# Moving the first list load of a routed layer ahead of the last scatters, and 4 KB runs for three input loads

## The chip, the core and the metric

One core of a Trainium2 chip runs the whole program. The metric is the device time of one execution in microseconds (us). TensorE (PE) does the matrix products, VectorE (DVE) and ScalarE (ACT) the elementwise work, GpSimd (POOL) issues the indirect transfers, and SyncE (SP) issues the ordinary ones. Each engine works through its own instructions in the order in which they were written, and waits where an operand isn't ready.

## The reference, cut to what matters

```python
p_packed = sm_attn(p, k, v)              # 8 batches x 8 heads, 576 keys, 32 packed rows, head 64
x = sm_attn(q, p_packed, p_packed)       # -> 4608 tokens x 512
h = np.maximum(x @ w_in, 0.0)            # dense layer, 2048 wide
x = (h * h) @ w_out
noisy = x @ w_gate + log1p(exp(x @ w_noise)) * noise   # 8 experts
top2 = argpartition(-noisy, 2)[:, :2]; top2_w = softmax of the two
for e in range(8):                       # routed layer, 1024 wide, two experts per token
    out[mask_e] += top2_w * (np.maximum(x[mask_e] @ w1[e], 0) @ w2[e])
```

`w_in` and `w_out` come as 64-bit floats and are decoded on the core into pairs of 32-bit numbers.

## The kernel before

**Stages.** The dense layer runs in 16 blocks `j` of 288 tokens (two blocks make a batch of 576), each in 16 steps `f` of 128 hidden columns. A step is six matmuls on PE (line 655), the squared ReLU on ACT and DVE (lines 659 to 683), and, two steps later, twelve matmuls of the second product (line 691). Its second operand `gl` is made by DVE (line 682). The routed layer follows in tiles: each expert has three (512, 384 and 256 tokens, with 64 more for four of the experts), and a tile has eight steps.

**Routing.** After each batch `route(k)` finds for every token its two experts and its place in each expert's list, and writes (token, weight) into the DRAM tensor `lst` with scatters: twelve for a batch, one after the other on POOL (line 627), each waiting until the one before has landed. The last batch is routed in two halves, `route(7)` and `route(8)`, of six scatters each. After batch 5 the fullest expert so far is named the first one, and its first list (512 places) is taken as full; its second list (384 places) is full after batch 6.

**Lists, gathers, transposes.** `load_groups(k)` reads list `k` in the order of the gathers (four transfers into `lg0`, line 794), `group_index` turns that into row numbers `gi0` on DVE (line 800), and `load_list` reads it with the weights (four transfers into `ls0`, line 788). `gather` reads 32 token rows by `gi0` with one indirect transfer on POOL (line 837), 16 of them for tile 0 and 12 for tile 1. `trans_a` turns the gathered rows on DVE (line 845), `trans_b` splits them into two parts on ACT and DVE (lines 853 and 854), and the tile's matmuls (line 863) read those.

**The order.** Blocks 0 to 14, with the decode of the weights, the attention and the routing of batches 0 to 6, are ordered by a planner (`schedule`). It takes each `unit` with its engine, cost and dependences; where PE would idle in the first 45 us it inserts small matmuls (line 1113). A scatter costs 1040 ns on POOL there, and a transfer lands 1200 + 900 ns later. From block 15 on the order is written out by hand (lines 1125 to 1242). In block 15, step 0 loads list 0 and computes its index, step `SPL` does the same for list 1; `G0` places the gathers of tile 0 at steps 1 to 7 and 9, `T0` its transposes at steps 8, 11, 12 and 13. The weights of the first expert arrive through a two-buffer tile `wst` (`wload` on SP, `wsplit` on ACT and DVE), one per step. `RP` and `RR` are the half steps of block 15 at which the pieces of the logits and of `route(7)` stand; `SPEC` does the same for `route(8)` in tile 0.

**Input loads.** A chunk of `w_in` (512 KB) is read as 512 runs of 1 KB, 16 KB apart; one of `w_out` as 128 runs of 4 KB. `q` (576 KB for a block) is read in runs of 1152 bytes from four distant planes, `v` (512 KB and a rest of 64 KB) in neighbouring runs of 1 KB, `kT` (576 KB) in runs of 4608 bytes. Chunks go through three buffers `st`; the first four are the ones that this text speaks of most.

Of the kernel before, what the change touches and what calls it, by code (L numbers as in the profile page):

```python
# [12 lines left out]
I32 = mybir.dt.int32  # L13
# [8 lines left out]
P = 128  # L22
B, H, S, D = 8, 8, 576, 64
NPK = 32
NT, DM, FF = B * S, H * D, 2048
E, F2 = 8, 1024
BLK = 288
NB = NT // BLK
# [1 line left out]
RT = BLK // QP  # L30
KC = 5
XB = 6
SPL = 7
YS = 3
GF = 2
GLEAD = 2
# [10 lines left out]
NFF = FF // P  # L47
# [10 lines left out]
DUE = 9  # L58
RING = 8
JA = 2  # L60
RP = [5, 8]
RR = [11, 11, 13, 14, 16, 18, 18, 20, 22, 24, 26, 28, 30]
SPEC = [4, 5, 6, 6, 7, 8, 9, 9, 10, 10, 11, 14, 15, 15, 16, 17]
TILES = ((P, P, P, P), (P, P, P), (P, P))
EXTRA = P // 2
# [14 lines left out]
JSPEC = {B - 3: SIZE[0], B - 2: SIZE[0] + SIZE[1]}  # L80
# [2 lines left out]
TERMS = ((0, 0), (0, 1), (1, 0))  # L83


def program(ctx, tc, qT, kT, v, pT, w_in, w_out, wg, wn, noise, w1, w2, out):
    nc = tc.nc
    ctx.enter_context(tc.manual_schedule())
    dram = ctx.enter_context(tc.tile_pool(name="dram", bufs=1, space=DRAM))
# [42 lines left out]
    ls0 = cst.tile([P, BASE[2], 2], I32, name="ls0")  # L132
    lg0 = cst.tile([P, 4 * BASE[2], 2], I32, name="lg0")
    gi0 = cst.tile([P, 4 * BASE[2]], I32, name="gi0")
# [50 lines left out]
    raw = {}  # L185

    def load_raw(n):
        kind, i = chunks[n]
        raw[n] = stg.tile([P, 512, 2], I32, name="st", bufs=STB)
        if kind:  # L190
            nc.sync.dma_start(raw[n].rearrange("p a b -> p (a b)"), w_out[P * i:P * i + P].bitcast(I32))
        else:
            nc.sync.dma_start(raw[n].rearrange("p (c f) b -> p c (f b)", c=4),
                              w_in[:, P * i:P * i + P].bitcast(I32).rearrange("(c p) f -> p c f", p=P))

    units = {}

    def unit(name, eng, fn, deps, cost=60, dma=0, psum=(), dense=0.98):
        units[name] = (eng, cost, deps, fn, dma, psum, dense)
# [72 lines left out]
    def part1(n):  # L272
        b, quad = n // 2, n % 2
        st = {}
# [7 lines left out]
        def u_v():  # L282
            if n in LENT:
                w = win[:, 2:, FF - 512:].rearrange("p a (c d) -> p a c d", c=2)
                st["v"] = [w[:, c // 2, c % 2] for c in range(4)] + [win[:, 2, FF - 768:FF - 512]]
                for a in range(2):
                    nc.sync.dma_start(w[:, a], v[b, quad, 256 * a:256 * a + 256].rearrange("(c p) d -> p c d", p=P))
            else:
                w = p1.tile([P, KC, 256], F, name="vq", bufs=1)
                st["v"] = [w[:, c] for c in range(KC)]  # L290
                nc.sync.dma_start(w[:, :4], v[b, quad, :512].rearrange("(c p) d -> p c d", p=P))
            nc.sync.dma_start(st["v"][4][:64], v[b, quad, 512:])

        def u_s():
            st["s"] = [side(f"s1{i}", [P, 288]) for i in range(2)]
# [56 lines left out]
        x, y = ("A", n), ("A", n - 1)  # L352
# [61 lines left out]
    def part2(j):  # L414
        b = j // 2
        st = {}

        def u_l():
            st["q"] = att.tile([P, 4, BLK], F, name="q", bufs=QB)
            nc.sync.dma_start(st["q"], qT[:, :, j * BLK:(j + 1) * BLK].rearrange("g p t -> p g t"))  # L420

        def u_s():
            st["s"] = [side(f"s2{r}", [P, BLK]) for r in range(2)]
            heads(b, st["s"], st["q"])

        def u_m():
            a = att.tile([P, 2 * BLK], F, name="a2", bufs=1)
            for r in range(2):
                nc.vector.transpose(a[:, r * BLK:(r + 1) * BLK], st["s"][r])
            a = st["a"] = a.rearrange("p (x k) -> p x k", k=NPK)  # L430
            m = att.tile([P, 2 * BLK // NPK], F, name="m2", bufs=2)
            nc.vector.tensor_reduce(m, a, axis=AX.X, op=OP.max)
            nc.vector.tensor_sub(a, a, m.unsqueeze(2).to_broadcast([P, 2 * BLK // NPK, NPK]))

        def u_e():
            nc.scalar.activation(st["a"], st["a"], AF.Exp, scale=SCALE)

        def u_n():
            s = att.tile([P, 2 * BLK // NPK], F, name="sm2", bufs=2)
            a = st["a"]  # L440
            nc.vector.tensor_reduce(s, a, axis=AX.X, op=OP.add)
            nc.vector.tensor_scalar(s, s, 1e-9, None, op0=OP.add)
            nc.vector.reciprocal(s, s)
            nc.vector.tensor_mul(a, a, s.unsqueeze(2).to_broadcast([P, 2 * BLK // NPK, NPK]))

        def u_t():
            st["aT"] = att.tile([P, 2, BLK], F, name="aT", bufs=1)
            nc.vector.transpose(st["aT"].rearrange("p d t -> p (d t)"), st["a"].rearrange("p x k -> p (x k)"))

        def u_h():  # L450
            for i in range(2):
                xT[j, i] = mo.tile([P, 2, BLK], FR, name=f"xT{i}", bufs=2)
            act_copy(xT[j, 0], st["aT"])

        def u_d():
            nc.gpsimd.tensor_sub(xT[j, 1], st["aT"], xT[j, 0].bitcast(F))  # L456

        x, prev = ("Q", j), ("Q", j - 1)
        unit(x + ("l",), "sp", u_l, [("Q", j - QB, "s")], dma=393216)
        unit(x + ("s",), "pe", u_s, [x + ("l",), prev + ("t",), ("A", 2 * b, "y"), ("A", 2 * b + 1, "y")], 560,  # L460
             psum=(x + ("m",),) * 2, dense=0.89)
        unit(x + ("m",), "dve", u_m, [x + ("s",), prev + ("t",)], 2400)
        unit(x + ("e",), "act", u_e, [x + ("m",)], 620)
        unit(x + ("n",), "dve", u_n, [x + ("e",)], 2050)
        unit(x + ("t",), "dve", u_t, [x + ("n",), prev + ("h",), prev + ("d",)], 680)
        unit(x + ("h",), "act", u_h, [x + ("t",), ("M", j - 2, NFF - 1, "1")], 620)
        unit(x + ("d",), "pool", u_d, [x + ("h",)], 1500)
# [40 lines left out]
    def route(k):  # L508
        r0, n = ROUTES[k]
        st = {}  # L510
# [121 lines left out]
        rest = [u1, u1b, u1c, u2, u2b, u3, u3b] + [sc(r, i) for r in range(n) for i in range(2)]  # L632
        if k < B - 1:
            p = ("R", 2 * k + 1, "l")
            for i, (fn, eng, c) in enumerate(((u1, "dve", 250), (u1b, "act", 2700), (u1c, "dve", 1500),
                                              (u2, "dve", 2200), (u2b, "dve", 1700), (u3, "pe", 100), (u3b, "dve", 2000))):
                unit(("U", k, i), eng, fn, [p, ("U", k - 1, 6 + 4 * RT)], c, psum=(("U", k, 6),) if i == 5 else ())
                p = ("U", k, i)
            for i in range(4 * RT):
                unit(("U", k, 7 + i), "pool", rest[7 + i], [p], 1040, dma=64)  # L640
                p = ("U", k, 7 + i)
        if k == len(ROUTES) - 1:
            rest.insert(7, u3c)
        return rest
# [104 lines left out]
    def expert(e):  # L749
        if e not in reg:  # L750
            reg[e] = nc.sync.value_load(ordi[:1, min(e, 1), e:e + 1], min_val=0, max_val=E - 1)
        return bass.ds(reg[e], 1)
# [32 lines left out]
    def load_list(k, es, dst):  # L785
        src, n, r = list_rows(k, es)
        for g in range(n // 32):
            nc.sync.dma_start(dst[32 * g:32 * g + 32, :, BASE[k]:BASE[k] + r], src[g])

    def load_groups(k, es, dst):  # L790
        l = lst.rearrange("(e s) w -> e s w", e=E)[es, START[k]:START[k] + SIZE[k]]
        l = l.rearrange("e (j b) w -> j e b w", j=32)
        for a in range(4):
            nc.sync.dma_start(dst[32 * a:32 * a + 32], l)

    def groups(k):
        return slice(4 * BASE[k], 4 * BASE[k] + SIZE[k] // 32)

    def group_index(dst, src):
        nc.vector.tensor_scalar(dst, src, 4.0, pq4, op0=OP.mult, op1=OP.add)  # L800

    def by_rank(src, n, out=None):
        t = m2["a"].tile([P, 4, P], F, name="xs", bufs=2).rearrange("p a b -> p (a b)")[:, :(E - 1) * n * E]
# [321 lines left out]
    for i, (kind, j, f) in list(enumerate(steps))[NS * NFF:]:  # L1125
# [15 lines left out]
        if kind == 0 and j == NB - 1:  # L1141
            if f >= LAG - 1:
                wload(0, f - LAG + 1)
            for k, sl in enumerate((0, SPL)):
                if f == sl:
                    load_groups(k, expert(0), lg0[:, groups(k)].unsqueeze(1))
                    group_index(gi0[:, groups(k)], lg0[:, groups(k), 0])
                    load_list(k, expert(0), ls0.unsqueeze(1))
            for t, r, x in G0.get(f, ()):
                gather(t, r, x, x + 2)  # L1150
            if f in T0:
                trans_a(0, T0.index(f))
# [15 lines left out]
        else:  # L1168
# [28 lines left out]
            elif j + 1 < len(tiles):  # L1197
                if (j, f) in LST:
                    for k in LST[j, f]:
                        b = groups(abs(k) % 8)  # L1200
                        i = min(abs(k) % 8, 2)
                        b = slice(b.start - 4 * BASE[i], b.stop - 4 * BASE[i])
# [10 lines left out]
                if (j, f) in LGI:  # L1213
                    for k in LGI[j, f]:
                        if k < 0:
                            b = slice(4 * BASE[2], NG)
# [3 lines left out]
                        else:  # L1220
                            b = groups(k)
                            rank_groups(k, b.start, NG if k == 2 else b.stop)
                n = len(rows(j + 1))
# [27 lines left out]
    with tc.For_i(0, n_over, 1) as j:  # L1251
        with tc.tile_pool(name="sb3", bufs=1) as sb, tc.tile_pool(name="ps3", bufs=1, space=PSUM) as ps:
# [12 lines left out]
            for r in range(2):  # L1265
                g = sb.tile([P, DM], F, name="g", bufs=2)
# [11 lines left out]
            for r in range(2):  # L1278
# [3 lines left out]
                y = sb.tile([P, DM], F, name="y", bufs=2)  # L1282
# [36 lines left out]
```

## Time and profile before

| | us |
|---|---|
| median of 3 runs | 1714.87 |
| range of the runs | 1714.64 to 1718.84 |
| the profiled execution | 1713.52 |
| its span in the trace | 1711.7 |

Times in the rows below are counted from the span's start. The profiled execution lies 1.35 us under the median and outside its span has 1.8 us. PE is busy for 96% of the span.

### The profile page before, as it was taken

The page shows a single profiled execution, that of the slowest core. Times are in us where ns is not written, and L with a number is a line of the kernel's source. Part 1 is how long each engine was busy: PE and PEld are TensorE (multiplying, and loading weights), DVE is VectorE, ACT ScalarE, POOL GpSimd, SP SyncE. Part 2 cuts the span into 40 slices and gives each one's busy share as a digit, 9 for nine tenths or more (in the row PEclk, how much of TensorE's full clock was granted, in tenths as well). Part 3 has the DMA queues.
Part 4 walks back from the last instruction along what each step waited for, and adds up shares of the span by engine and source line. Part 5 has one row for each costly group of instructions (what it writes and reads, how often), then busy time and mean ns, then how long its engine had stood idle before and what let it go on. Part 6 is the DMA issues. An engine that isn't in the chain of part 4 may idle for free. (4 is left out here: it accounts for less than half of the span.)

```text
span 1711.7 us, 28563 instructions
## 1 busy us (share of the span) xinstructions
PE 1650.4 (96%) x11110; PEld 1430.0 (84%) x11110; DVE 877.4 (51%) x2040; ACT 640.9 (37%) x1372; POOL 537.0 (31%) x500
## 2 busy tenths in 40 slices
PE   8999999999999999995899799999999999999996
PEld 6669898989898998995788588888888888888886
DVE  6993757566665757572645544334343343433321
ACT  4775545344444444442623223222222232322211
POOL 0000020302011111204415636535365363645611
PEclk9999999999999999997999899999999999999998
DMA  8653132232322112102415535334253343534312
GB/s 243 189 156 79 29 95 70 69 97 69 96 67 79 48 53 58 29 15 59 95 24 122 112 58 120 74 83 96 62 104 84 73 108 68 111 75 92 69 25 32
DMA packets 143664, 140.80 MB, mean 82 GB/s; under 512 B 33071, under 2 KB 111919, under 8 KB 143527
## 3 DMA queue, kind: packets, MB, share of 16 engines
q1 hardware_dynamic: 120295, 100.05, 20.9%
q0 software_dynamic: 23232, 38.90, 13.3%
q8 instruction: 88, 1.44, 0.4%
q14 instruction: 49, 0.40, 0.1%
HBM read 99.71 MB, written 39.19 MB: 81 GB/s over the span
## 5 line engine op out<-in xcount | busy, mean ns | idle before, releaser
L691 PE MATMUL acc<-gh,wo 128*128 128x288 f32 x2048 | 426.1, 301 | 17.6 <-DVE x2T L698 17.6
L691 PEld LDWEIGHTS acc<-gh,wo 128*128 128x128 f32 x2048 | 330.0, 190 | 49.3 <-issue 22.4
L837 POOL DMA_INDIRECT xg<-x2d,gi x296 | 295.6, 999 | 107.6 <-issue 98.8
L870 DVE SCALAR_TENSOR_TENSOR hl<-ph,hh 128x512 fp32r<-128x512 f32 (+3 forms) x184 | 105.7, 575 | 433.7 <-ACT hh L869 433.6
L691 PE MATMUL acc<-gl,wo 128*128 128x288 f32 x1024 | 303.3, 296 | 1.6 <-DVE gl L682 1.5
L869 ACT ACTIVATE hh<-ph 128x512 fp32r<-128x512 f32 (+3 forms) x184 | 92.7, 504 | 484.8 <-PE ph L863 484.8
L655 PE MATMUL ph<-xT,ring 128*128 128x288 f32 x1536 | 246.4, 301 | 0.7 <-POOL xT L456 0.5
L627 POOL DMA_INDIRECT lst<-ent,pi x96 | 90.9, 947 | 483.9 <-DVE pi L606 248.0
L863 PE MATMUL ph<-ring,wb 128*128 128x512 f32 (+3 forms) x1152 | 225.0, 345 | 8.6 <-ACT ring L104 8.6
L655 PEld LDWEIGHTS ph<-xT,ring 128*128 128x128 f32 x1536 | 215.4, 189 | 19.2 <-ACT g L662 8.1
L892 POOL DMA_INDIRECT out<-y,ls x76 | 123.7, 1627 | 325.2 <-DVE y L889 158.4
L863 PE MATMUL ph<-ring,wo 128*128 128x512 f32 (+3 forms) x1152 | 222.0, 341 | 1.9 <-DVE hl L870 1.9
L863 PEld LDWEIGHTS ph<-ring,wb 128*128 128x128 f32 x1152 | 195.8, 189 | 32.6 <-ACT ring L104 9.0
L863 PEld LDWEIGHTS ph<-ring,wo 128*128 128x128 f32 x1152 | 194.0, 188 | 24.6 <-DVE hl L870 2.4
L691 PEld LDWEIGHTS acc<-gl,wo 128*128 128x128 f32 x1024 | 194.4, 190 | 2.9 <-DVE gl L682 2.9
L880 PE MATMUL acc<-wo,hh 128*128 128x512 f32 (+1 forms) x608 | 191.3, 396 | 0.0
L662 ACT ACTIVATE g<-ph 128x288 f32<-128x288 f32 x256 | 104.2, 407 | 221.0 <-PE ph L655 213.1
L880 PE MATMUL acc<-wb,hh 128*128 128x512 f32 (+1 forms) x576 | 179.5, 393 | 0.0
L677 DVE TENSOR_TENSOR g<-g 128x288 f32<-128x288 f32 x208 | 98.2, 472 | 129.3 <-ACT gh L668 128.9
L682 DVE TENSOR_TENSOR gl<-g,gh 128x288 fp32r<-128x288 f32 x256 | 123.4, 482 | 51.5 <-ACT gh L104 35.7
L880 PEld LDWEIGHTS acc<-wo,hh 128*128 128x128 f32 (+1 forms) x608 | 110.5, 185 | 22.7 <-issue 0.5
L880 PEld LDWEIGHTS acc<-wb,hh 128*128 128x128 f32 (+1 forms) x576 | 105.0, 185 | 20.6
(203 smaller groups left out, 1785.9 us busy)
## 6 DMA issues: line engine op xcount, KB each, us to landing
wst<-w SPq DMA_DIRECT2D x128, 256.0 KB, 3.0
out<-zero SPq DMA_DIRECT2D x37, 256.0 KB, 4.2
q<-qT SPq DMA_DIRECT2D x16, 576.0 KB, 4.7
x2d<-x2s SPq DMA_DIRECT2D x64, 144.0 KB, 2.7
kq<-kT SPq DMA_DIRECT2D x15, 576.0 KB, 3.8
st<-w_in SPq DMA_DIRECT2D x16, 512.0 KB, 7.7
st<-w_out SPq DMA_DIRECT2D x16, 512.0 KB, 4.2
vq<-v SPq DMA_DIRECT2D x15, 512.0 KB, 4.1
```

The lines of the kernel that those rows point to most:

```text
L627: nc.gpsimd.indirect_dma_start(out=lst, out_offset=bass.IndirectOffsetOnAxis(ap=st["pi"][:, r, k:k + 1], axis=0), in_=st["ent"][:, r, k], ...
L655: nc.tensor.matmul(ph, w[:, a, d], xT[j, b][:, d], start=n == 0, stop=n == 5)
L662: nc.scalar.activation(g, ph, AF.Relu)
L677: nc.vector.tensor_mul(g, g, g)
L682: nc.vector.tensor_sub(gl, g, gh.bitcast(F))
L691: nc.tensor.matmul(acc[j][d], wo[:, f, b, d * P:(d + 1) * P], g[a], start=f == 0 and n == 0, stop=f == NFF - 1 and n == 2)
L837: nc.gpsimd.indirect_dma_start(out=g[:, x], out_offset=None, in_=src, in_offset=bass.IndirectOffsetOnAxis(ap=idx, axis=0))
L863: nc.tensor.matmul(ph, wblock(e, f, a)[:, c], xt[t][b][:, c, :n], start=i == 0, stop=i == 11)
L869: nc.scalar.activation(hh, ph, AF.Relu)
L870: nc.vector.scalar_tensor_tensor(hl, ph, 0.0, hh.bitcast(F), op0=OP.max, op1=OP.subtract)
L880: nc.tensor.matmul(acc["e", t, r], h[a][:, o:o + n], wblock(e, 8 + f, b).rearrange("p c f -> p (c f)"), start=first and i == 0, stop=last ...
L892: nc.gpsimd.indirect_dma_start(out=out, out_offset=bass.IndirectOffsetOnAxis(ap=sl[:, 0:1], axis=0), in_=y, in_offset=None, compute_op=OP.add)
```

## The change

Three things change. **Lists:** the load of list 0 leaves step 0 of block 15 and becomes three units of the planner, behind the last scatter of batch 5 and ahead of the first scatter of batch 6: groups and list on SP, the index on DVE. The first scatters of batch 6 wait for both loads. List 1 is loaded at step 8 instead of 7, and its index stands two steps behind its load. **Routing slots:** the pieces of `route(7)` are spread anew over block 15. **Layouts:** the host lays out `w_in`, `v` (all but its last 64 rows) and `q` so that each partition reads one run of 4 KB (`q`: 4608 bytes).

```diff
-SPL = 7
+SPL = 8
-RP = [5, 8]
-RR = [11, 11, 13, 14, 16, 18, 18, 20, 22, 24, 26, 28, 30]
+RP = [5, 7]
+RR = [8, 8, 11, 12, 14, 21, 22, 23, 25, 26, 27, 29, 30]
...
-            nc.sync.dma_start(raw[n].rearrange("p (c f) b -> p c (f b)", c=4),
-                              w_in[:, P * i:P * i + P].bitcast(I32).rearrange("(c p) f -> p c f", p=P))
+            nc.sync.dma_start(raw[n].rearrange("p a b -> p (a b)"), w_in[i].bitcast(I32))
...
-                nc.sync.dma_start(w[:, :4], v[b, quad, :512].rearrange("(c p) d -> p c d", p=P))
-            nc.sync.dma_start(st["v"][4][:64], v[b, quad, 512:])
+                nc.sync.dma_start(w[:, :4], v[b, quad])
+            nc.sync.dma_start(st["v"][4][:64], v5[b, quad])
...
-            nc.sync.dma_start(st["q"], qT[:, :, j * BLK:(j + 1) * BLK].rearrange("g p t -> p g t"))
+            nc.sync.dma_start(st["q"], qT[j])
...
-                unit(("U", k, 7 + i), "pool", rest[7 + i], [p], 1040, dma=64)
+                unit(("U", k, 7 + i), "pool", rest[7 + i], [p] + [("L", k - 1, y) for y in "gl"], 1040, dma=64)
                 p = ("U", k, 7 + i)
+        if k == min(JSPEC):
+            unit(("L", k, "g"), "sp", lambda: first_groups(0), [p], 400, dma=64)
+            unit(("L", k, "l"), "sp", lambda: first_list(0), [("L", k, "g")], 400, dma=64)
+            unit(("L", k, "i"), "dve", lambda: first_index(0), [("L", k, "g")], 100)
...
+    def first_groups(k):
+        load_groups(k, expert(0), lg0[:, groups(k)].unsqueeze(1))
+
+    def first_index(k):
+        group_index(gi0[:, groups(k)], lg0[:, groups(k), 0])
+
+    def first_list(k):
+        load_list(k, expert(0), ls0.unsqueeze(1))
...
-            for k, sl in enumerate((0, SPL)):
-                if f == sl:
-                    load_groups(k, expert(0), lg0[:, groups(k)].unsqueeze(1))
-                    group_index(gi0[:, groups(k)], lg0[:, groups(k), 0])
-                    load_list(k, expert(0), ls0.unsqueeze(1))
+            if f == SPL:
+                first_groups(1)
+                first_list(1)
+            if f == SPL + 2:
+                first_index(1)
```

## Rows read from the trace of the kernel before

**Rows 1.** The page's first part: engine, busy us, share, instructions.

```profile
PE 1650.4 (96%) x11110; PEld 1430.0 (84%) x11110; DVE 877.4 (51%) x2040; ACT 640.9 (37%) x1372; POOL 537.0 (31%) x500
```

**Rows 2.** Waits of the whole span: waiter, releaser, us in total, times, longest.

```profile
PE acc L691 <- DVE x2T L698: 17.6, 1, 17.6
PE ph L863 <- ACT ring L104: 8.6, 1, 8.6
...
PE ta L317 <- ACT pk L104: 2.9, 1, 2.9
```

**Rows 3.** Timeline of PE, block 15: start, us, engine, line, operation, count, [idle before].

```profile
776.13 0.96 PE L655 MATMUL ph<-xT,ring 128*128 128x288 f32 x6
778.53 0.96 PE L655 MATMUL ph<-xT,ring 128*128 128x288 f32 x6
...
797.49 0.85 PE L691 MATMUL acc<-gh,wo 128*128 128x288 f32 x2 [17.61 <-DVE x2T L698]
...
801.07 1.81 PE L655 MATMUL ph<-xT,ring 128*128 128x288 f32 x6
...
824.45 0.26 PE L577 MATMUL rk<-os,low 96*96 96x24 bf16 x1 [5.34 <-DVE os L571]
...
841.97 2.91 PE L863 MATMUL ph<-ring,wo 128*128 128x512 f32 x12
```

**Rows 4.** Busy time by stretch: length, PE, PEld, DVE, ACT, POOL, clock, DMA share, GB/s.

```profile
780.00:800.00 20.00, 2.51 (x13) 2.23 (x17) 1.69 (x5) 0.85 (x2) 6.68 (x8) 0.58 0.08 21
```

**Rows 5.** Timeline of DVE in block 15.

```profile
796.47 0.23 DVE L800 TENSOR_SCALAR gi<-lg,pq 128x16 int32<-128x16 int32 x1 [19.89 <-DMA lg<-lst]
...
838.97 0.70 DVE L845 STREAM_TRANSPOSE xs<-xg 128x512 f32<-128x512 f32 x1
```

**Rows 6.** Timeline of SP: the load of list 0's groups.

```profile
792.89 2.25 SPq L794 DMA_DIRECT2D lg<-lst  x4
```

**Rows 7.** Timeline of POOL: scatters of batches 5 to 7, gathers of tiles 0 and 1.

```profile
670.34 0.92 POOL L627 DMA_INDIRECT lst<-ent,pi  x1 [51.54 <-DVE sm L337]
...
704.04 0.92 POOL L627 DMA_INDIRECT lst<-ent,pi  x1 [1.69 <-DMA lst<-ent,pi]
...
790.83 0.92 POOL L627 DMA_INDIRECT lst<-ent,pi  x1 [1.40 <-DMA lst<-ent,pi]
797.51 0.97 POOL L837 DMA_INDIRECT xg<-x2d,gi  x1 [5.76 <-DVE x2T L698]
...
816.66 0.94 POOL L837 DMA_INDIRECT xg<-x2d,gi  x1 [0.30 <-issue]
829.79 1.14 POOL L627 DMA_INDIRECT lst<-ent,pi  x1 [12.19 <-DVE pi L606]
...
855.98 0.94 POOL L837 DMA_INDIRECT xg<-x2d,gi  x1 [0.30 <-issue]
876.87 0.94 POOL L627 DMA_INDIRECT lst<-ent,pi  x1 [19.95 <-DVE key L611]
```

**Rows 8.** The gathered tile `xg`, 790 to 860 us: ns min/median/max, landing after issue.

```profile
L837 POOL DMA_INDIRECT xg<-x2d,gi x28: 940/945/1471, 797.5 to 856.0; - x28
...
DMA to landing us min/median/max: 2.5/3.1/4.4
```

**Rows 9.** Busy time of the first stretch (columns as in rows 4).

```profile
0.00:20.00 20.00, 18.55 (x229) 14.40 (x230) 11.77 (x38) 7.54 (x18) 1.44 (x12) 1.00 0.96 294
```

**Rows 10.** Timeline of ACT: the fourth chunk of `w_in`.

```profile
22.59 0.66 ACT L210 ACTIVATE dec_t<-st 128x512 f32<-128x512 f32 x1 [4.76 <-DMA st<-w_in]
```

**Rows 11.** The page's transfers: count, KB each, median us from issue to landing.

```profile
q<-qT SPq DMA_DIRECT2D x16, 576.0 KB, 4.7
...
kq<-kT SPq DMA_DIRECT2D x15, 576.0 KB, 3.8
...
st<-w_out SPq DMA_DIRECT2D x16, 512.0 KB, 4.2
vq<-v SPq DMA_DIRECT2D x15, 512.0 KB, 4.1
```

More of the change, by code (lines that the diff above doesn't have):

```diff
@@ L83, with program @@
 TERMS = ((0, 0), (0, 1), (1, 0))
-def program(ctx, tc, qT, kT, v, pT, w_in, w_out, wg, wn, noise, w1, w2, out):
+def program(ctx, tc, qT, kT, v, v5, pT, w_in, w_out, wg, wn, noise, w1, w2, out):
     nc = tc.nc
@@ L285, in u_v @@
                 st["v"] = [w[:, c // 2, c % 2] for c in range(4)] + [win[:, 2, FF - 768:FF - 512]]
-                for a in range(2):
-                    nc.sync.dma_start(w[:, a], v[b, quad, 256 * a:256 * a + 256].rearrange("(c p) d -> p c d", p=P))
+                nc.sync.dma_start(w, v[b, quad].rearrange("p (a c) d -> p a c d", a=2))
             else:
@@ L1299 @@
             pT[:, :, h, :, c, h] = pp[:, :, c, h].transpose(0, 1, 3, 2)
+    v4 = v.reshape(B, 2, 4, S, D).transpose(0, 1, 3, 2, 4).reshape(B, 2, S, 256)
     a = {
-        "qT": q.transpose(1, 3, 0, 2).reshape(4, P, NT),
+        "qT": q.transpose(1, 3, 0, 2).reshape(4, P, NB, BLK).transpose(2, 1, 0, 3),
         "kT": k.reshape(B, 2, 2, 2, S, D).transpose(0, 1, 3, 5, 2, 4).reshape(B, 2, P, 2, S),
-        "v": v.reshape(B, 2, 4, S, D).transpose(0, 1, 3, 2, 4).reshape(B, 2, S, 256),
+        "v": v4[:, :, :512].reshape(B, 2, 4, P, 256).swapaxes(2, 3),
+        "v5": v4[:, :, 512:],
         "pT": pT.reshape(B, 2, P, 2, 64),
-        "w_in": i["moe_w_in"].view(np.int64),
+        "w_in": i["moe_w_in"].view(np.int64).reshape(4, P, NFF, P).transpose(2, 1, 0, 3).reshape(NFF, P, 512),
         "w_out": i["moe_w_out"].view(np.int64),
```

## The prediction

> **What bounds the kernel now.** I read the page's first part, then the waits of PE, then the timelines of the engines around the longest of them. PE is busy for 96% of the span [rows 1], so time can only be won where PE stands still or runs slowly. Its waits show three places worth naming: 17.6 us in front of line 691, 8.6 us in front of line 863, and 2.9 us behind ACT in the first 25 us [rows 2].
>
> The first lies in block 15. A step there takes 2.40 us (776.13 to 778.53), and at the third step PE stops until 797.49 [rows 3]. The releaser that the row names, a DVE copy, is only next in line: DVE itself stood for 19.89 us in front of the index of list 0, and that waited for the transfer of the list [rows 5]. SP issued it at 792.89 [rows 6], as soon as the last scatter of batch 6, issued at 790.83, had landed [rows 7]. The index waits for twelve serial scatters, and `gl`, on which PE's second product hangs, is queued behind it on DVE. The stop costs more than its length: the mean granted clock of 780 to 800 us is 0.58 [rows 4], so PE was at 1.2 GHz for most of it, and behind it six matmuls take 1.81 us instead of 0.96 [rows 3]. A second stop of 5.34 us at 824.45 ends on DVE's routing of the half batch [rows 3]. Tile 0 starts at 841.97 [rows 3]. At full pace 14 steps after 778.53 and the logits' matmuls (two groups, 0.5 us each at the planner's price) it would start at 778.53 + 33.6 + 1.0 = 813.1. Block 15 thus loses **28.9 us**.
>
> **Part 1, the lists.** The change takes the wait away from block 15: list 0 is read behind the scatters of batch 5, whose last is issued at 704.04, and the scatters of batch 6 begin later by over 50 us in either order. The eight issues on SP (2.25 us for four, [rows 6]) and the index (0.23 us, [rows 5]) fall into the gap on POOL between the two batches, and I cost them at nothing. If that cover were gone, the loads would add some 2 x 2.25 + 3.6 = 8 us to the scatter chain (3.6 is from the issue in [rows 6] to the index in [rows 5]). Queued behind the waiting load on SP are x2 stores and block loads that are due tens of us later.
>
> With the index gone, POOL is late next. Its queue is in order, and the scatters of batch 6 hold it until 790.83 + 0.92 = 791.75, in both kernels. The gathers then begin 0.3 us later, at 792.05, not at 797.51 [rows 7]. The sixteen take 15 intervals of (816.66 - 797.51) / 15 = 1.277 us, so the last is issued at 811.2 [rows 7] and lands 3.1 us later [rows 8], at 814.3. In the trace of before the last transpose starts at 838.97 [rows 5] and tile 0 at 841.97 [rows 3]; I take these 3.0 us, though PE was not waiting there, since DVE and ACT also have a step's `gl`, a split and a copy to do in between. Tile 0 then starts at **817.3** and block 15 gives back 841.97 - 817.3 = **24.7 us**. PE still loses about 4 of the 28.9, late in the block, in stops too short to bring the pace of 801.07 back.
>
> Bounds: no more than 28.9, if nothing of the gathers is seen. At the other end every gather takes the longest time of the rows, 1.47 + 0.30, and the last lands after 4.4 us [rows 8]: 15 x 0.49 + 1.3 = 8.7 us later, a gain of 16.0. I stay at 24.7, since of 28 gathers the median is 0.945 us, 5 ns above the least [rows 8].
>
> Here a page speaks against the change. The gathers now run beside the routing's DVE work. The Trainium skill, SBUF — State Buffer, section "SBUF: two separate sides", says that descriptors of transfers issued from GpSimd cannot be written while DVE runs an instruction in a two-port mode. It would push this part towards its lower bound; the median gather of rows 8, beside the same kinds of DVE work, doesn't show it, its longest one may.
>
> **Part 2, the routing slots and list 1.** The matmul that waited 5.34 us moves from half step 18 to 21, 1.5 steps or 3.6 us later, while the pieces ahead of it start 1.5 steps sooner; this stop is gone, and its gain is inside the 24.7, as is that of the slow pace. List 1's load, eight issues on SP at step 8, comes when the scatters have just landed; behind it stands one `wst` load, held by some 4 us, which the two steps of slack (4.8 us) between load and use cover. The index two steps later finds it landed. A gather of tile 1 or a scatter of `route(7)` may now be late. POOL's work from the first gather to the last of tile 1 is 855.98 - 797.51 - 12.19 (idle) = 46.3 us [rows 7], and would end at 838.3. The next scatters, of `route(8)`, hang on PE's tile 0 and move up from 876.87 to about 852 [rows 7]. POOL has about 13 us in hand, so all that follows, the 8.6 us stop at tile 3 included, moves up whole.
>
> **Part 3, the layouts.** The transfers are nearly saturated only at the start: 0.96 of the first 20 us at 294 GB/s, 5.9 MB [rows 9]. Later PE hides them. The fourth chunk of `w_in` comes through that queue; ACT waits 4.76 us for it [rows 10], and PE 2.9 us behind ACT [rows 2]. Whether long runs are faster has two pairs of rows: `q` (1152 bytes, far apart) lands in 4.7 us and `kT` (4608 bytes, same size) in 3.8, a fifth less; `v` (1 KB, neighbouring) lands in 4.1 and `w_out` (4 KB, same size) in 4.2, no difference [rows 11]. The runs of `w_in` are far apart, like those of `q`. Four chunks of it and one block of `q`, 2.7 of the 5.9 MB, take 9.1 us of the 20; a fifth less is **1.7 us**, and PE's 2.9 shrink by it. Bounds: 0, and 2.9. Nothing else at the start moves, since PE's warming matmuls keep their place and number.
>
> The page against this is DMA: Bandwidth & Descriptors of the Trainium skill, section "Specifications": from 512 B a transfer runs at line rate. By it runs of 1 KB lose nothing and this term is 0. The pair `v` and `w_out` agrees, the pair `q` and `kT` doesn't.
>
> **The sum.** 24.7 + 1.7 = 26.4 us. The profiled execution would go from 1713.5 to 1687.1 us; the median of the runs shown lies 1.35 above the profiled execution, so I forecast 1714.87 - 26.4 = **1688.5 us**.
>
> **The rivals.** *Runs of 4 KB bring nothing.* For it: the pair `v` and `w_out`; against it: the pair `q` and `kT`. Only part 1 remains: 1690.2 us. By the page's 512-byte rule it is so.
>
> *The gathers take the place of the index.* POOL's intervals grow to the bound of part 1, because the gathers run beside more DVE work and beside the loads of `wst`. For it: the longest gather; against it: the median. Gain 16.0 + 1.7: 1697.2 us.
>
> *Everything goes.* Neither gathers nor ACT are seen, and the start gives 2.9: 28.9 + 2.9, 1683.1 us.
>
> *Slower: the index blocks DVE in the planned part.* The planner sets the index where its own clock has the load landed; on the chip DVE would stop there until it has. The scatters of batch 5 run from 670.34 to 704.04, and the list would land at about 704.04 + 2.1 (792.89 less 790.83, [rows 6, 7]) + 3.6 = 709.7. PE can run two steps, 4.8 us, without DVE. If the index stood where those scatters begin, DVE would wait 39 us, PE 34.5, and 34.5 - 26.4 = 8.1 us would be lost: 1723.0 us. It decides from an index 31.2 us too early (26.4 + 4.8). Against it: the planner gives each scatter 1.04 + 2.1 = 3.14 us, twelve 37.7 us, and the rows have 33.7 us for eleven intervals, 36.8 for twelve; the two clocks differ by 1 us, not 31. An index 25 to 31 us early would give about no change.
>
> **How the numbers follow.** Forecast 0.50, no gain from the runs 0.24, late gathers 0.12, everything goes 0.05, index blocks DVE by over 31 us 0.05, about no change 0.04. The likeliest is the forecast. The range of 1682 to 1699 takes in the first four, 0.91, and so the bounds of both unknown terms; the rest of the width is not needed for 8 in 10, but a new order of the planner's units may shift any of them by a us or two. A measurement of this kernel tells 0.3%, about 5 us, from no change: faster 0.90, within 0.3% 0.05, slower 0.05.
>
> **What would show it.** In the trace of after: the index of list 0 on DVE before 761 us with a wait under 3 us; no stop of PE over 5 us between 770 and 820 us; the first gather at about 792 us (less what the start gives) and tile 0 at 815 to 820; the wait of ACT for the fourth chunk near 3 us; the 8.6 us stop of tile 3 still there, moved up whole. It is wrong if the first gather comes later than the last scatter by more than 2 us, if the stop at tile 3 grows, or if DVE waits long for the index in the planned part.

## The result, and the profile after

| | before | after |
|---|---|---|
| median, us | 1716.31 | 1696.99 |
| range of four runs, us | 1714.64 to 1718.84 | 1691.83 to 1699.73 |
| ratio of the medians, 95% interval | | 0.9883 [0.9852, 0.9913] |
| the profiled execution, us | 1713.52 | 1691.83 |
| start of block 15 (first matmul behind its wait for `xT`) | 773.76 | 771.90 |
| start of tile 0 | 841.97 | 818.66 |
| start of tile 3 | 963.95 | 941.54 |

The change takes 19.3 us off the median; I had forecast 26.4. The two profiled executions lie 21.7 us apart (their spans 21.6), and the profiled one of after is the fastest of its four, so the trace shows after at its best. By the table, 1.9 us of the span come from ahead of block 15 and 21.4 from block 15 (68.21 to 46.76); 0.9 are given back between tile 0 and tile 3 and 0.8 behind it.

The waits of PE in after. The columns are total, count and longest, in us:

```profile
PE ph L874 <- ACT ring L104: 7.0, 1, 7.0
PE ph L657 <- ACT g L664: 4.3, 4, 1.7
PE ph L874 <- DVE hl L881: 2.5, 1, 2.5
PE ta L315 <- ACT pk L104: 1.3, 1, 1.3
```

Of the three places of [rows 2], the stop of 17.6 us is gone, and so is the one of 5.34 [rows 3]. The stop at tile 3 (now line 874) is still there, 7.0 us in place of 8.6, and so is the one in the tile ahead of it, 2.5 us at 928.90 in place of 1.9 at 951.30. New is a sum of 4.3 us in front of line 657: PE waits for ACT's `g`. The table by stretch (busy time of PE, weight load, DVE, ACT, POOL, then granted clock, DMA share, GB/s) answers [rows 4]:

```profile
780.00:800.00 20.00, 19.26 (x142) 18.59 (x142) 11.78 (x43) 14.36 (x30) 8.75 (x10) 1.00 0.48 110
800.00:820.00 20.00, 16.61 (x107) 14.44 (x106) 13.75 (x31) 12.81 (x29) 15.43 (x16) 1.00 0.46 129
```

PE is busy and stays at 2.4 GHz, where it stood at a mean of 0.58 before. The DMA share of 0.48 is new too, and matters below. The index of list 0, which waited 19.89 us [rows 5], now stands on DVE in the planned part:

```profile
709.80 0.23 DVE L802 TENSOR_SCALAR gi<-lg,pq 128x16 int32<-128x16 int32 x1
```

It has no wait at all, 50 us ahead of batch 6's first scatter at 760.02. On POOL (answering [rows 7]) the last three of those scatters, the first gather and the sixteenth:

```profile
785.86 0.92 POOL L625 DMA_INDIRECT lst<-ent,pi  x1 [3.23 <-DMA lst<-ent,pi]
789.31 0.99 POOL L625 DMA_INDIRECT lst<-ent,pi  x1 [2.53 <-DMA lst<-ent,pi]
792.87 0.92 POOL L625 DMA_INDIRECT lst<-ent,pi  x1 [2.57 <-DMA lst<-ent,pi]
794.10 0.98 POOL L848 DMA_INDIRECT xg<-x2d,gi  x1 [0.30 <-issue]
...
814.03 0.94 POOL L848 DMA_INDIRECT xg<-x2d,gi  x1 [0.30 <-issue]
```

The gathers do follow the last scatter at once. But that scatter is late: in before the scatters of block 15 waited 1.4 us for each other, one 2.14, and the last was issued at 790.83; here the last three wait 2.5 to 3.2 us. SP shows what was not there before:

```profile
781.93 1.86 SPq L712 DMA_DIRECT2D x2d<-x2s  x4
784.06 15.13 SPq L765 DMA_DIRECT2D wst<-w  x6
799.43 1.91 SPq L796 DMA_DIRECT2D lg<-lst  x4
```

In before SP's next issue after 738.58 was the list's load at 792.89 [rows 6]: the waiting load had held back the `x2` stores (a block's tokens, written to DRAM for the gathers; then at 803.07) and the loads of the first expert's weights (from 797.41). With the load gone they run beside the scatters.

Tile 0 starts 4.6 us after the sixteenth gather's issue. PE's three stops over 0.5 us inside block 15, and that start:

```profile
795.84 1.07 PE L657 MATMUL ph<-xT,ring 128*128 128x288 f32 x6 [0.74 <-ACT g L664]
803.03 1.06 PE L657 MATMUL ph<-xT,ring 128*128 128x288 f32 x6 [1.71 <-ACT g L664]
812.53 1.06 PE L657 MATMUL ph<-xT,ring 128*128 128x288 f32 x6 [1.67 <-ACT g L664]
818.66 3.20 PE L874 MATMUL ph<-ring,wo 128*128 128x512 f32 x12
```

What ACT waited for in the last two is on DVE and ACT:

```profile
801.30 0.71 DVE L856 STREAM_TRANSPOSE xs<-xg 128x512 f32<-128x512 f32 x1 [2.15 <-DMA xg<-x2d,gi]
802.05 0.63 ACT L104 ACTIVATE ring<-xs 128x512 fp32r<-128x512 f32 x1 [2.21 <-DVE xs L856]
...
810.80 0.71 DVE L856 STREAM_TRANSPOSE xs<-xg 128x512 f32<-128x512 f32 x1
811.55 0.63 ACT L104 ACTIVATE ring<-xs 128x512 fp32r<-128x512 f32 x1 [2.73 <-DVE xs L856]
812.09 0.39 ACT L664 ACTIVATE g<-ph 128x288 f32<-128x288 f32 x1
```

ACT's queue is in order: its copy of a transposed row waits for DVE, and `g`, for which PE waits, is queued behind the copy. The first of the two hangs on a gather's landing (DVE waited 2.15 us). The second does not: ten small instructions of the half batch's routing (lines 582 to 604, 808.71 to 810.80) stand ahead of the transpose.

### The profile page after: what moved, and what is told of

The parts are those of the page before. It is cut to its first block, busy times and chain, and to the rows that moved or that the text cites. A ratio compares the mean times of both kernels' runs of the same rounds, so it can differ in the third digit from the quotient of the medians.

```text
span 1690.1 us, 28554 instructions
## 1 busy us (share of the span) xinstructions
PE 1649.8 (98%) x11103; PEld 1427.6 (84%) x11110; DVE 877.8 (52%) x2040; ACT 640.8 (38%) x1372; POOL 543.3 (32%) x500
## 5 line engine op out<-in xcount | busy, mean ns | idle before, releaser
L848 POOL DMA_INDIRECT xg<-x2d,gi x296 | 299.6, 1012 | 102.3 <-issue 86.7
L891 PEld LDWEIGHTS acc<-wo,hh 128*128 128x128 f32 (+1 forms) x608 | 110.6, 186 | 22.9 <-issue 0.5
```

The source lines that it names most:

```text
L848: nc.gpsimd.indirect_dma_start(out=g[:, x], out_offset=None, in_=src, in_offset=bass.IndirectOffsetOnAxis(ap=idx, axis=0))
L891: nc.tensor.matmul(acc["e", t, r], h[a][:, o:o + n], wblock(e, 8 + f, b).rearrange("p c f -> p (c f)"), start=first and i == 0, stop=last ...
```

## The experiments

Three series ran, each on another chip. The kernel before took 1744.87 us in the first, 1716.71 in the second and 1718.07 in the third, so kernels of different series are compared by their ratios to it, and traces by times counted from the start of block 15.

| kernel | series | median, us | ratio to before, 95% interval |
|---|---|---|---|
| layouts_only | 1 | 1743.18 | 0.9989 [0.9974, 1.0004] |
| no_layouts | 1 | 1716.25 | 0.9842 [0.9824, 0.9860] |
| old_slots | 1 | 1720.11 | 0.9861 [0.9842, 0.9881] |
| after_again | 1 | 1716.34 | 0.9828 [0.9806, 0.9849] |
| after_third | 2 | 1694.57 | 0.9872 [0.9856, 0.9888] |
| x2_late | 2 | 1694.90 | 0.9872 [0.9857, 0.9887] |
| wst_once | 2 | 1694.49 | 0.9873 [0.9858, 0.9889] |
| interleave | 2 | 1690.51 | 0.9844 [0.9830, 0.9857] |
| interleave_again | 3 | 1690.88 | 0.9848 [0.9830, 0.9865] |
| turn_first | 3 | 1695.41 | 0.9866 [0.9844, 0.9888] |
| spread | 3 | 1690.83 | 0.9845 [0.9828, 0.9861] |
| spread_x2 | 3 | 1688.11 | 0.9827 [0.9811, 0.9843] |

### The parts of the change by themselves

**layouts_only** is before with the three layouts, **no_layouts** is after without them. The lines that differ are those of the diff under "The change" that read `w_in`, `v` and `q`.

> The kernel before with the 4 KB layouts of w_in, v and q alone; block 15 as before. Theory (the start queue moves sooner): PE's stop behind ACT at 20 to 24 us shrinks from 2.9 to about 1.3 us, tile 0 starts 1.5 to 2 us sooner, the time is 1.5 to 2.5 us below before. Rival (runs of 1 KB lose nothing): the stop stays 2.9 us and the time is that of before within 0.5 us. In both, the 17.6 us stop of block 15 stays.

> The changed kernel with the old layouts of w_in, v and q. Theory: block 15 alone brings 21.4 us in the profiled execution (tile 0 from 841.97 to about 820.5), so 19 to 22 us below before; the start is as before (stop of 2.9 us). Rival (the layouts also relieve the transfers in block 15, where q is no longer loaded): then more than 3 us of the gain are lost with them.

**old_slots** is after with the old places of the routing pieces:

```diff
-RP = [5, 7]
-RR = [8, 8, 11, 12, 14, 21, 22, 23, 25, 26, 27, 29, 30]
+RP = [5, 8]
+RR = [11, 11, 13, 14, 16, 18, 18, 20, 22, 24, 26, 28, 30]
```

> The changed kernel with the half steps of route(7) as before (11, 11, 13, 14, 16, 18, 18, 20 and on). Theory of the prediction (the new slots remove the 5.3 us stop in front of the rk matmul): that stop comes back in part, 2 to 5 us, with a stretch at the lower clock behind it, and part of it is hidden since PE waits for the gathers later in any case: 1 to 5 us slower than the changed kernel. Rival (the stop came from the index of list 1 waiting on DVE, which now stands two steps behind its load): the stop stays away, within 1 us of the changed kernel.

> The changed kernel again, beside the others on the same chip: 1690 to 1700 us. Theory: executions differ by the landing times of the scatters of batch 6 and of the gathers that follow, so that tile 0 starts between 816 and 824 us, and everything behind it moves with it. Rival: tile 0 starts at 818 to 819 us as in the first trace, and the difference arises later, at tile 3 (a stop of 9.5 us in the first trace).

Measured: the lists and the slots carry the change. Without the layouts the ratio is 0.9842, with them 0.9828, and the two intervals overlap; the layouts alone bring 1.7 us, with an interval that contains none. No_layouts lies 28.6 us below before, more than the 19 to 22 that I had expected; on this chip every kernel is slower, and the last section comes back to it. The traces say the same in another way. These are ACT's waits for the fourth chunk in layouts_only and in after_again, both with runs of 4 KB:

```profile
20.75 0.66 ACT L209 ACTIVATE dec_t<-st 128x512 f32<-128x512 f32 x1 [3.18 <-DMA st<-w_in]
```

```profile
22.14 0.66 ACT L209 ACTIVATE dec_t<-st 128x512 f32<-128x512 f32 x1 [4.50 <-DMA st<-w_in]
```

Over the twelve traces with the 4 KB layouts (after and all experiments but no_layouts) this wait is 3.10 to 4.59 us, with a mean of 3.85; over the two with the old ones it is 4.76 [rows 10] and 3.92. PE's stop behind it is 1.3 to 2.8 against 2.9 and 2.1. The first trace of after had the shortest wait of all. So what one pair of traces showed as 1.9 us is mostly the scatter of executions: the means differ by 0.5 us, and what the layouts are worth stays open between nothing and some 2 us.

The slots are worth 3.8 us here (1720.11 against 1716.34). In old_slots the stop that I had put to them is back, and so is its releaser:

```profile
805.92 0.26 PE L575 MATMUL rk<-os,low 96*96 96x24 bf16 x1 [5.24 <-DVE os L569]
```

The expectation for after_again was too optimistic on that chip: tile 0 came at 835.88, not 816 to 824. What held it is told in the last section.

### What held the scatters

**after_third** repeats after. **x2_late** moves the `x2` stores of block 14 half a block back:

```diff
-    at_slot(HS * (NB - 1) + RP[0], seq(lambda: x2_turn(NB - 2), lambda: x2_store(NB - 2)))
+    at_slot(HS * (NB - 1) + RP[0], lambda: x2_turn(NB - 2))
+    at_slot(HS * (NB - 1) + 21, lambda: x2_store(NB - 2))
```

**wst_once** leaves out five weight loads:

```diff
+        if e == 0 and 0 < i < 6:
+            wst[e, i] = wst0[0]
+            return
```

> The changed kernel again, as the measure for the three others of this series: all of them are compared with it by their ratios to the kernel before, and by the moments of their traces counted from the start of block 15. Expected as in the first trace of after: the last three scatters of batch 6 wait 2.5 to 3.2 us each for the one before to land, first gather some 22 us after block 15 begins, sixteenth gather 19.9 us behind the first, tile 0 4.6 us behind that. If the chip shows stops that nothing in the profile ends (as in the series before), tile 0 comes up to 17 us later.

> After, with one thing moved: the four x2 stores of block 14, which SP issues at 781.93 in after between batch 6's last scatters, are issued half a block later. Theory (transfers that the freed SP queue sets loose lengthen the scatters' landings): the 3.23 us wait in front of the third last scatter goes back to about 1.4, the last scatter and the first gather come 1.8 us sooner, tile 0 up to 1.8 us sooner. If the loads of wst are what lengthens the landings, the waits keep their 2.5 us and nothing moves. Rival (the landings are longer by themselves in this stretch, whatever SP does): all three waits stay at 2.5 to 3.2, time as after within 1 us.

> After, with five of the first expert's six weight loads left out (its tiles 1 to 5 use chunk 0 in their place, so that part of the output is not the reference's): SP's loads of 1 MB that run beside batch 6's scatters and the gathers are gone. Theory (those loads lengthen the landings): the waits of 2.5 us in front of the last two scatters return to about 1.4, the gathers' intervals of 1.329 to 1.28, the first gather 2.2 us and the sixteenth 3 us sooner, tile 0 up to 3 us sooner. Rival (not those loads, but the x2 stores): the 3.23 stays and the others too; nothing moves before tile 0. Rival two (neither): as after.

POOL's last three scatters of batch 6 and the first gather, first in after_third:

```profile
788.09 0.92 POOL L625 DMA_INDIRECT lst<-ent,pi  x1 [3.20 <-DMA lst<-ent,pi]
791.63 0.92 POOL L625 DMA_INDIRECT lst<-ent,pi  x1 [2.62 <-DMA lst<-ent,pi]
796.02 0.92 POOL L625 DMA_INDIRECT lst<-ent,pi  x1 [3.47 <-DMA lst<-ent,pi]
797.24 0.98 POOL L848 DMA_INDIRECT xg<-x2d,gi  x1 [0.30 <-PE acc L693]
```

in x2_late:

```profile
783.44 0.92 POOL L625 DMA_INDIRECT lst<-ent,pi  x1 [1.65 <-DMA lst<-ent,pi]
786.55 0.92 POOL L625 DMA_INDIRECT lst<-ent,pi  x1 [2.19 <-DMA lst<-ent,pi]
788.86 0.92 POOL L625 DMA_INDIRECT lst<-ent,pi  x1 [1.40 <-DMA lst<-ent,pi]
790.09 0.98 POOL L848 DMA_INDIRECT xg<-x2d,gi  x1 [0.31 <-issue]
```

and the three scatters in wst_once:

```profile
788.37 0.92 POOL L625 DMA_INDIRECT lst<-ent,pi  x1 [3.51 <-DMA lst<-ent,pi]
790.72 1.11 POOL L625 DMA_INDIRECT lst<-ent,pi  x1 [1.43 <-DMA lst<-ent,pi]
793.22 0.92 POOL L625 DMA_INDIRECT lst<-ent,pi  x1 [1.39 <-DMA lst<-ent,pi]
```

This settles the late scatter. Take the weight loads away, and the last two waits fall to the 1.4 us of before while the third last keeps its 3.5; move the stores away, and that one falls to 1.65. The one long wait left in x2_late, 2.19, stands beside a weight load that SP issued at 783.03. Each wait belongs to the transfers that run beside it, and the rival "the landings are longer by themselves" falls. From the start of block 15 the first gather comes after 23.66 us in after_third, 20.31 in wst_once and 19.01 in x2_late.

But the time does not follow. x2_late has its sixteenth gather (809.47) 38.4 us after block 15's start where after_third needs 43.5; tile 0 comes after 46.9 us against 48.1, and the medians are 1694.90 and 1694.57. Five microseconds of sooner gathers bring one microsecond in the trace, none against the first trace of after (46.8), and none in the time, though the trace of x2_late is of the fastest of its four executions (1688.57, the others 1694.31 and more). Wst_once tells the same: its sixteenth gather comes after 39.2 us, tile 0 after 47.0, and its median is 1694.49. My expectation "up to 1.8 us sooner" still took the gathers for what tile 0 waits for. In x2_late PE's last stop reads:

```profile
811.20 1.06 PE L657 MATMUL ph<-xT,ring 128*128 128x288 f32 x6 [2.09 <-ACT g L664]
...
818.01 2.91 PE L874 MATMUL ph<-ring,wo 128*128 128x512 f32 x12
```

Behind it, in 812 to 816 us, the mean granted clock is 0.61: having stood for 2 us, PE runs the next step partly at 1.2 GHz. After_third shows the same at another place, a stop of 3.47 us at 806.88 behind a late gather, and then 0.57 in 807 to 811 us. In the trace of after the clock stays at 1.00 behind its stops of 1.71 and 1.67 us.

### What ends block 15

**interleave** moves the last eight scatters of batch 6 from the planner into half steps 2 to 9 of block 15 and puts one gather of tile 0 behind each, so that POOL issues a gather while a scatter lands:

```diff
+    for x, u in enumerate(R[B - 2][7 + KEEP:]):
+        at_slot(HS * (NB - 1) + 2 + x, u)
+        at_slot(HS * (NB - 1) + 2 + x, lambda x=x: gather(0, x // 4, x % 4, x % 4 + 1))
```

> After, with the last eight of batch 6's scatters moved into half steps 2 to 9 of block 15, each followed by one of tile 0's first eight gathers, so that POOL issues a gather while a scatter lands. Theory (what is late next is POOL's serial order: scatters, then sixteen gathers): the eight gathers lie in waits of 1.4 to 3 us that POOL has anyway; only eight remain behind the last scatter, the sixteenth gather is issued about 8 x 1.33 = 10.6 us sooner if the scatters end as in after, tile 0 no longer waits for a gather and starts at PE's own pace, 4 to 6 us sooner: time 4 to 6 us (0.3%) below after. Rival (PE, ACT and DVE set the end of block 15 by themselves): gathers land sooner, tile 0 and the time stay within 1.5 us of after. Rival two (each scatter starts only behind a gather and its landing grows, so the chain ends later and list 1 with it): the last scatter over 8 us later, time above after.

> The interleaved kernel a second time, as the measure for the others of this series and to see whether its 4 us against after are more than scatter of the runs (0.9844 against 0.9872 of the kernel before). If they are: a ratio of 0.983 to 0.986, upper end of the interval below 0.9872. If not: 0.9865 or more. In the trace as the first time: sixteenth gather issued some 34 us after block 15's start, tile 0 at 48 to 49 us after it, with a stop of about 2 us in front of the last step but one.

The gathers did what they should: the sixteenth is issued 34.3 us after the start of block 15, not 43.5. The last scatter comes 22.9 us after that start (22.4 in after_third), so rival two falls. Tile 0 is no sooner for it, 48.7 and 48.3 us in the two traces, with the 2 us stop in place:

```profile
814.27 1.06 PE L659 MATMUL ph<-xT,ring 128*128 128x288 f32 x6 [2.08 <-ACT g L666]
821.06 2.23 PE L876 MATMUL ph<-ring,wo 128*128 128x512 f32 x9
```

So the rival (PE, ACT and DVE set the end) holds for block 15. All the same the time is 4.1 us below after_third; their intervals just touch, at 0.9856 to 0.9857. In the third series after itself did not run; there interleave_again has the ratio 0.9848, again below the 0.9872 of after_third, and 4.5 us less than turn_first, whose ratio is that of after. Where these 4 us are, one profile each can't say: the two traces of interleave begin block 15 at 772.36 and 770.78 (after 771.90 and 773.58) and need 120.8 and 121.5 us from tile 0 to tile 3 (after 122.9 and 122.4), some 1.2 and 1.5 us on the mean. The first is no larger than the scatter between two traces of one kernel (1.6 and 1.7 us); the second is, but x2_late, without the interleaving, has 120.8 as well. This stays open.

**turn_first** leaves the gathers alone and issues a row's transpose ahead of the routing piece of the same step:

```diff
+        if kind == 0 and j == NB - 1 and f in T0:
+            trans_a(0, T0.index(f))
         for x in work.get(2 * i, ()):
             x()
...
-            if f in T0:
-                trans_a(0, T0.index(f))
```

> After, with the transpose of each of tile 0's rows issued on DVE ahead of the routing piece of the same step, not behind it (it matters in step 11, where nine routing instructions of 0.17 to 0.36 us, from 808.71 to 810.80 in after, stand ahead of the transpose, ACT's copy of it waits 2.73 us, and ACT's g that PE waits for stands behind that copy). Theory (PE's stop of 1.67 us in front of step 14 comes by this way, DVE routing to DVE transpose to ACT copy to ACT g): ACT's wait goes from 2.7 to about 0.7, the stop of 1.67 to under 0.3, tile 0 1 to 1.6 us sooner counted from block 15's start (46.8 to about 45.5), time 1 us below after, too little for the interval. Rival (the gather of that row is what is late): the transpose waits for xg and the stop stays.

DVE and ACT of turn_first at the second and the fourth row:

```profile
810.64 0.70 DVE L856 STREAM_TRANSPOSE xs<-xg 128x512 f32<-128x512 f32 x1
811.55 0.62 ACT L104 ACTIVATE ring<-xs 128x512 fp32r<-128x512 f32 x1
...
819.79 0.71 DVE L856 STREAM_TRANSPOSE xs<-xg 128x512 f32<-128x512 f32 x1 [1.87 <-DMA xg<-x2d,gi]
820.54 0.63 ACT L104 ACTIVATE ring<-xs 128x512 fp32r<-128x512 f32 x1 [2.58 <-DVE xs L856]
821.52 1.84 PE L874 MATMUL ph<-ring,wo 128*128 128x512 f32 x6 [1.60 <-ACT g L664]
```

ACT's wait of 2.73 us and PE's stop in front of step 14 are gone, as the theory says. In their place DVE waits 1.87 us for the last row's gather, and PE 1.60 us in front of tile 0, which comes 47.7 us after the block's start; the time is that of after (ratios 0.9866 and 0.9872). Not all of this comes from the edit: at the first row, where after stood for 1.71 us, this trace has a stop of 2.48 behind a later gather, and a clock of 0.66 in 806 to 810 us. The gathers and the ring of ACT and DVE (the transpose on DVE, its copy on ACT, then `g` on ACT, for which PE waits) thus end within some 2 us of each other: whichever is shortened, the other shows. That is why x2_late, interleave and turn_first, each right about its own wait, start tile 0 hardly sooner. Up to here this is read from traces; the next two kernels test it.

**spread** is interleave with the transposes moved to steps away from the routing piece, **spread_x2** adds the later stores of x2_late:

```diff
-T0 = [8, 11, 12, 13]
+T0 = [6, 9, 12, 13]
```

> Interleaved, and tile 0's four transposes moved from steps 8, 11, 12, 13 to 6, 9, 12, 13, away from the routing piece of step 11 and out of two of the neighbouring steps; their gathers have landed by then. Theory (what ends block 15 is the ring of ACT and DVE in the steps with a transpose, 3.05 us each against PE's 2.40, and the routing piece in it): the stop of 2.08 us in front of step 14 goes, at most one of 0.7 to 1 us is left in front of step 15 or tile 0; tile 0 at 45.5 to 46.5 us after block 15's start, not 48.7; time 2 to 3 us below the interleaved kernel. Rival (the late loads of the weights hold ACT, 2.73 us in the interleaved trace, and so PE): stops of 1 us and more stay, tile 0 at 48, time as interleaved.

> As spread, and the four x2 stores of block 14 half a block later, as in x2_late, where the last three scatters then waited 1.4 to 2.2 us and not 2.6 to 3.5. Theory (block 15 no longer hangs on scatters or gathers): the scatters end 2 to 4 us sooner, and tile 0 and the time stay within 1 us of spread. Rival (list 1 and the weight loads queued behind it on SP still hang on the scatters): with the scatters 2 to 4 us sooner ACT's waits for the weights shrink, and tile 0 comes 1 us or more sooner than in spread.

Now both limits are shortened. Tile 0 in spread and in spread_x2:

```profile
816.40 3.22 PE L876 MATMUL ph<-ring,wo 128*128 128x512 f32 x12
```

```profile
814.54 3.22 PE L876 MATMUL ph<-ring,wo 128*128 128x512 f32 x12
```

Counted from block 15's start this is 46.6 us in spread, where interleave_again has 48.3, and 44.4 in spread_x2. The stop of 2 us is gone in both; the longest ones left are 1.31 and 0.91. The theory of the ring is right about this stop, but 46.6 is no better than the 46.8 of the first trace of after, and only spread_x2 starts tile 0 clearly sooner than every kernel before it. Spread's time (1690.83) is that of interleave_again (1690.88), and the 2 to 3 us that I expected did not come. Its trace is of its fastest execution (1688.62), that of interleave_again is of a middle one, so the 1.7 us between the traces may be scatter in part. Spread_x2 is 2.7 us faster than spread, with ranges of 1685.66 to 1688.89 and 1688.62 to 1692.23, and about as much as its tile 0 is sooner. I had given that to the rival (the weights' loads hang on the scatters). ACT's longest wait for a weight doesn't tell, 2.06 us in spread and 2.08 in spread_x2, but an earlier one does. Here is ACT at the same weight, first in spread, then in spread_x2:

```profile
787.41 0.63 ACT L106 ACTIVATE wo<-wst 128x512 fp32r<-128x512 f32 x1 [2.00 <-DMA wst<-w]
```

```profile
785.69 0.61 ACT L106 ACTIVATE wo<-wst 128x512 fp32r<-128x512 f32 x1
```

In spread the `x2` stores stand ahead of a weight's load in SP's queue, which issues it 12.44 us after the block's start (782.21); in spread_x2 it goes out after 8.74 us (778.88), and ACT doesn't wait. Counted from the block's start ACT is 2.1 us sooner there (15.55 against 17.64), and tile 0 keeps that, 2.2 us sooner. So a weight's load is the path, as the rival says, but what holds this one is the stores ahead of it on SP, and not a scatter. Spread_x2 has the lowest time of this study, 0.9827 of before in its series; after has 0.9872 in the second series, and 0.9828 on the slower chip of the first.

## Why the prediction was right, and where it was off

**The number.** 1696.99 us lies in the range of 1682 to 1699, but near its end, 8.5 us above the forecast. The gain is 7.1 us less than forecast: 3.3 are missing in block 15, 1.7 are given back behind the start of tile 0, the start gives 0.2 more, and the other 2.3 are there because the profiled execution of after lies further below its median than that of before. In after_third only 0.3 us are given back behind the start of tile 0, so the 1.7 are mostly scatter.

**What bounded the kernel** was read rightly. The wait for list 0 was the long one; with it gone PE keeps its clock at 1.00, and block 15 is 21.4 us shorter.

**Part 1: the term that was mis-sized is block 15's 24.7 us; it measured 21.4.** The failing step is "the scatters of batch 6 hold it until 790.83 + 0.92 = 791.75, in both kernels". Counted from block 15's start, the last scatter came 3.9 us later than that (792.87 against 788.97, with the 1.86 us by which the block began sooner). I had looked at what stood behind the waiting load on SP and found it due "tens of us later"; I did not ask what these transfers would do to the scatters once they ran beside them. Two smaller terms add up otherwise: the gathers' intervals are 1.329 us, not 1.277, which is 0.8 over fifteen, and from the sixteenth gather to tile 0 it takes 4.6 us, not 6.1. 3.9 + 0.8 - 1.5 = 3.2 of the 3.3 us missed.

That sum is right in its figures, but its last step was right by luck. I let tile 0 hang on the last gather plus 6.1 us, "though PE was not waiting there". The experiments show two limits close together, the gathers and the ring of ACT and DVE in the steps with a transpose (in after 3.03 us from 812.53 to the next start of line 657, and 3.10 from there to tile 0, where PE's own step is 2.40). Had the scatters kept to time, tile 0 would have come at most about 1 us sooner and not 3.9: x2_late and wst_once have it 46.9 and 47.0 us after the block's start, the two traces of after 46.8 and 48.1.

**The page against part 1** (the Trainium skill, SBUF — State Buffer, "SBUF: two separate sides") would have made the gathers slower beside DVE's work. Most of the sixteen in after take 0.94 to 0.98 us and the longest 1.46, as in [rows 8]. In wst_once, with the same DVE work but five weight loads fewer, all sixteen take 0.94 to 1.00 us at an interval of 1.257, so no run here shows the rule at work.

**Part 2** came as said: the stop of 5.34 us is gone, old_slots brings it back as 5.24, and it is worth 3.8 us there. The load of list 1 holds the weights' queue for 4 us (799.43 to 803.61), and the two steps of slack just cover it: ACT waits 0.72 us for the weight behind it.

**Part 3: the 1.7 us are not shown.** The trace of after had 1.86 us, and the wait that I named fell to 3.10, as forecast; twelve traces with the layouts put it at 3.85 on the mean. The failing step is "a fifth less", taken from one pair of landings. In after `w_in` landed in 6.7 us at the median and `q` in 4.1; in after_third, the same kernel, in 7.9 and 4.6, where before has 7.7 and 4.7. The rule of the Trainium skill (DMA: Bandwidth & Descriptors, "Specifications") that from 512 B a transfer runs at line rate gave this term nothing. The traces don't contradict it.

**The rivals.** *Runs of 4 KB bring nothing* is not excluded. *The gathers take the place of the index* is right in part, by the scatters ahead of them more than by their own intervals, and its 1697.2 us is nearest to the median by luck: it stands for gathers at intervals of 1.77 us, and they have 1.329. *Everything goes* and *the index blocks DVE* are out: 4.3 us of stops are left, and the index has no wait.

**The marks.** The index ahead of 761 us without a wait, no stop of PE over 5 us in 770 to 820 and ACT's wait near 3 us came as written. The stop at tile 3 moved up by 22.4 us, where tile 0 moved by 23.3, and is 1.6 us shorter. The first gather (794.10) was 3.9 us later than the start allows, and tile 0 fell into its 815 to 820.

## What to carry to other kernels

When a wait is taken out of an in-order queue, list what that queue then issues sooner, and look at which serial chains are landing beside it: here stores and weight loads set free on SP lengthened the waits for three scatters from 1.4 us to between 2.5 and 3.5, and in spread the stores also held up a weight's load by 3.7. Before a single chain is given the end of a stage, ask what ends within 2 us of it, since shortening one limit by 5 or 9 us, as x2_late and interleave do, may move the end by one or by none. And a gain of 1 to 2 us read from one pair of traces needs more traces than two.

## What the runs showed of the hardware

The chip of the first series ran the same kernels some 20 to 30 us slower than the others. Its traces show PE stops that nothing in the profile ends; in after_again:

```profile
806.72 1.05 PE L657 MATMUL ph<-xT,ring 128*128 128x288 f32 x6 [2.68 <-issue]
810.82 0.40 PE L693 MATMUL acc<-gh,wo 128*128 128x288 f32 x1 [1.32 <-issue]
817.22 0.40 PE L693 MATMUL acc<-gh,wo 128*128 128x288 f32 x1 [1.75 <-issue]
```

Such stops sum up to 12 us in that trace. At the same time SP, whose four issues of a list take 1.83 to 1.91 us in after, is slow too:

```profile
802.83 5.80 SPq L796 DMA_DIRECT2D lg<-lst  x4
811.47 7.81 SPq L790 DMA_DIRECT2D ls<-lst  x4
```

Layouts_only, with none of the list change, has as many (11.9 us, from 809 us on), so the change doesn't cause them; in the other two series and the first pair none is longer than 0.2 us. Their cause stays open, and so does what part they have in the change being worth 28.5 us there and 19.3 to 22.1 elsewhere. For their sake only ratios to the kernel before are compared across series.
